# Four blocks of 32 array columns in place of two of 64 in the last FFN

## The chip, the cores and the metric

The kernel runs on one core of one Trainium2 chip. The metric is the device time of one execution in microseconds. Three runs of the kernel before gave 2269.03, 2269.31 and 2272.66 us; their median, 2269.31, is the time before.

## What is computed

The reference has two parts, all in fp32 at the outside: a long convolution whose filter comes from a small network, and a feed-forward network (FFN) that takes the maximum of three products.

```python
h_filt = (np.maximum(pos_emb @ w1, 0.0) @ w2) * np.exp(-0.01 * np.arange(S))[:, None]
y = irfft(rfft(x * v, n=2 * S) * rfft(h_filt, n=2 * S), n=2 * S)[:S]   # along S, for each batch
x = (x * y).reshape(B * S, 128)
h = np.maximum(np.maximum(x @ moe_w1, x @ moe_w2), x @ moe_w3)
out = h @ moe_w_out
```

There are 4 batches of S = 12544 positions and 128 channels; the FFN has 768 hidden units.

## The kernel before, in words

**The work.** The Fourier transforms are done as matrix products with tables. The filter's spectrum comes first, with batch 0; from then on the convolution of one batch runs beside the FFN of the batch before it. The FFN of the last batch has no convolution beside it any more. It is the part that the change touches, and it is called the last FFN here.

**The FFN.** A batch is cut into 32 tiles of N = 392 positions. For each tile the last stage of the inverse transform (`t_last`, L747-764) makes the 128 x 392 convolution result in PSUM by products with 49 columns each, and VectorE multiplies it by x into `gt`. Then, for each of the six groups of 128 hidden units, an up step (`up`, L766-775) makes two 128 x 392 products in two PSUM banks (tile name `hps`). The weights were changed beforehand to w2 - w1 and w3 - w1, so ScalarE takes relu of the first product, VectorE the maximum of that and the second (`hid`); the part x @ w1 @ w_out comes back as a product with `lin`. In batches 0 to 2 `down` (L777-789) multiplies by w_out.

**The last FFN** (the loop at the end of the kernel, and `products`, L823-882) takes tiles in pairs and saves products by a Strassen-like scheme over seven products: GpSimd makes sums of hidden tiles (`sum_`, L803), VectorE makes sums of weights once, and the small function `mm` (L832-836) issues the products. There a stationary operand has 64 columns, and it is used for both halves of a moving operand of 392 columns: the first half goes into the lower 64 output partitions, the second into the upper 64. `ORDER` fixes which up step comes when, `SUMS` and `LAG` place sums and products some steps later; `stream` holds what is due at which step. The loop issues an up step, then what is due. The last stage of the tiles two ahead is issued in the steps j = 5 and j = 8 of each pair. The first two tiles of the last FFN get their last stage earlier, while the other FFNs still run, and its first up step is issued before the loop too.

**How products use the array.** TensorE's array has 128 columns. `halves_mm` (L152-157) cuts a product with 128 output partitions into two instructions with 64 columns each, which use different column blocks of the array; up, down, the last stage and some products of the convolution all go through it, so their instructions all stand under L156. `mm` does the like at L834. A program's fp32 product shows in the trace as two weight loads (PEld) and two matmuls (PE), which are called records or passes here. Every product has its own weight load, and the queue of TensorE runs them in the program's order as far as their waits allow.

**Queues.** In the last FFN the loads are issued by SP, the stores by GpSimd (L858), four for each half of the output of a tile pair.

Of the kernel before, what the change touches and what calls it, by code (L numbers as in the profile page):

```python
# [16 lines left out]
P = 128  # L17
# [74 lines left out]
def kernel(  # L92
# [15 lines left out]
    nc = tc.nc  # L108
# [40 lines left out]

    copies = (nc.scalar.copy, nc.vector.tensor_copy)  # L150

    def halves_mm(out, lhsT, rhs, start, stop):  # L152


        for h in range(2):
            nc.tensor.matmul(out[64 * h:64 * h + 64], lhsT[:, 64 * h:64 * h + 64], rhs,  # L156
                             start=start, stop=stop, skip_group_check=True)

    def first_halves(ps, lhs, table, dsts, engines):
# [17 lines left out]
    def second(ps, w, g):  # L177

        for k in range(2):
            for r in range(2):  # L180
                halves_mm(ps[:, (2 * k + r) * D:(2 * k + r + 1) * D], w[:, k, r, :],
                          spec[:, 2 * g + k, r, :], k == 0 and r == 0, True)
# [127 lines left out]
    def warm_up(n):  # L310

        ps = next(turns_)
        for _ in range(n):
            halves_mm(ps[:, 0:256], warm[:, 0:P], warm[:], True, True)
# [279 lines left out]
    def g_third(g):  # L594
        w, ab = ws.pop((g, 1)), abs_.pop(g)
        ps = state["cv"][1].tile([P, 512], FP32, tag="cv", name="ps3")
        for k in range(2):
            for q in range(2):
                halves_mm(ps[:, (2 * k + q) * D:(2 * k + q + 1) * D], w[:, k, q, :],
                          ab[:, k, q, :], k == 0 and q == 0, True)  # L600
        if g < NK - 2:
            zs = state["cv"][0].tile([P, 2, 256], FP32, tag="z", name="zs", bufs=2)
        else:
            zs = lwp.tile([P, 2, 256], FP32, tag="w1", name="zs")
        nc.scalar.copy(zs[:].rearrange("p k f -> p (k f)"), ps[:])
        nc.sync.dma_start(
            zd[0][2 * g:2 * g + 2].rearrange("k c t f -> (c t) k f"), zs[:])
# [158 lines left out]
    def up(i, f, tag="hid", bufs=3):  # L766
        rhs = gs[i][:].rearrange("d p n -> d (p n)")
        h = (hidp if tag == "hid" else lp).tile([P, N], FP32, tag=tag, name="hid", bufs=bufs)
        pa = next(hbanks)
        halves_mm(pa[:, 0:N], w_sb[1][:, f * P:(f + 1) * P], rhs, True, True)  # L770
        nc.scalar.activation(h[:], pa[:, 0:N], Relu)  # L771
        pb = next(hbanks)
        halves_mm(pb[:, 0:N], w_sb[2][:, f * P:(f + 1) * P], rhs, True, True)
        nc.vector.tensor_tensor(out=h[:], in0=h[:], in1=pb[:, 0:N], op=ALU.max)  # L774
        return h

    def down(i, f, h):  # L777
        if f == 0:
            pos_[i] = ops.tile([D, 512], FP32, tag="ops", name="ops")
            halves_mm(pos_[i][:, 0:N], lin[:], gs[i][:].rearrange("d p n -> d (p n)"), True,  # L780
                      False)
        halves_mm(pos_[i][:, 0:N], wo_sb[:, f, :], h[:], False, f == NF - 1)
        if f < NF - 1:
            return
        gs.pop(i)
        o = op_.tile([D, 4, NB], FP32, tag="o", name="ot")
        nc.scalar.copy(o[:].rearrange("d p n -> d (p n)"), pos_.pop(i)[:, 0:N])  # L787
        dst = outT.rearrange("d (p b n) -> d p b n", b=B, n=NB)[:, 4 * i[1]:4 * i[1] + 4, i[0], :]
        nc.gpsimd.dma_start(dst, o[:])  # L789
# [5 lines left out]
    H2 = N // 2  # L795
# [27 lines left out]
    def products(b, i, h, X, Y):  # L823

        m1, m2 = lin[:, 0:64], lin[:, 64:128]
        first, second_ = gs[b, i], gs[b, i + 1]
        t = {}

        def new(name, bufs=1):
            return lp.tile([P, H2], FP32, tag=name, name=name, bufs=bufs)  # L830

        def mm(ps, w, rhs, start):  # L832
            for c in range(2):
                nc.tensor.matmul(ps[64 * c:64 * c + 64, 0:H2], w, rhs[:, H2 * c:H2 * c + H2],  # L834
                                 start=start, stop=True, skip_group_check=True)

        def place(name):

            if name[0] != "c":
                t[name] = new(name)  # L840
                return t[name][:]
            n, m = int(name[1]) - 1, int(name[2]) - 1
            if m not in t:
                t[m] = lp.tile([P, 2, H2], FP32, tag="o", name="o", bufs=2)
            return t[m][:, n]

        def copied(name, ps):
            nc.scalar.copy(place(name), ps[:, 0:H2])

        def added(name, a, ps):  # L850
            nc.vector.tensor_tensor(out=place(name), in0=t[a][:], in1=ps[:, 0:H2], op=ALU.add)  # L851

        def stored(m):
            dst = outT.rearrange("d (p b n) -> d p b n", b=B, n=NB)
            for n in range(2):
                for c in range(2):
                    at = 4 * (i + n) + 2 * c
                    nc.gpsimd.dma_start(  # L858
                        dst[64 * m:64 * m + 64, at:at + 2, b, :],
                        t[m][64 * c:64 * c + 64, n].rearrange("d (q n) -> d q n", q=2))  # L860

        plan = (
            (X, "h11", wo_sb[:, 0:NC, 0:64], True, None, [(copied, "p1", X)], None),
            (Y, "s2", tw[:, 0], True, None, [(added, "u2", "p1", Y)], None),
            (X, "h12", wo_sb[:, NC:, 0:64], False, (m1, first), [(copied, "c11", X)], None),
            (Y, "s3", tw[:, 1], False, (m2, second_), [(added, "u3", "p1", Y)], None),
            (X, "h21", wo_sb[:, 0:NC, 64:128], True, None, [(added, "c22", "u3", X)], None),
            (Y, "h22", tw[:, 2], True, (linx[:], second_), [(added, "c21", "u3", Y)],
             (stored, 0)),
            (X, "h12", wo_sb[:, NC:, 64:128], False, (m2, first), [(added, "c12", "u2", X)],  # L870
             (stored, 1)),
        )
        out = []
        for ps, name, w, start, extra, then, store in plan:
            for j in range(NC):
                out.append([lambda ps=ps, name=name, w=w, start=start, j=j: mm(
                    ps, w[:, j, :], h[name, j][:], start and j == 0)])
            if extra:
                out.append([lambda ps=ps, extra=extra: mm(ps, extra[0], extra[1][:].rearrange("d p n -> d (p n)"), False)])
            out[-1] += [lambda a=a: a[0](*a[1:]) for a in then]  # L880
            out[-1].append(store)
        return out
# [306 lines left out]
    for n, (b, i) in enumerate(tiles[:LAST]):  # L1189
# [21 lines left out]
        for f in range(NF):  # L1211
# [9 lines left out]
            h = up((b, i), f)  # L1221
# [18 lines left out]
    for l in late:  # L1240
        down(*l)
    conv.close()


    lp = ctx.enter_context(tc.tile_pool(name="lp", bufs=1))
# [20 lines left out]
    for i in range(0, NT, 2):  # L1266
        h = {}
        X, Y = banks if i % 4 == 0 else banks[::-1]
        for j, (name, f) in enumerate(ORDER):
# [6 lines left out]
            if step > 2 and weights:  # L1276
                out, a1, a2 = weights.pop(0)
# [59 lines left out]
```

## Time and profile before

| | us |
|---|---|
| time of the runs: median (lowest to highest of 3) | 2269.31 (2269.03 to 2272.66) |
| span of the profiled execution, first to last instruction | 2267.5 |
| first product of the last FFN to TensorE's last product | 1850.3 to 2260.1 |
| busy in that stretch: TensorE / its weight loads | 409.7 / 252.3 |
| busy in that stretch: VectorE / ScalarE / GpSimd | 196.5 / 104.4 / 265.1 |

The page gives the profiled execution only by its span; the median of the runs lies 1.8 us above it.

How to read the lines: a row of a group or of the timeline has the line of the kernel, the engine, the operation, the tile written and the tiles read, the shape, and the count. A shape such as `128*64 128x392 f32` is 128 rows and 64 columns of the array, and a moving operand of 128 partitions and 392 columns. PE stands for matmuls, PEld for weight loads. A row of the timeline begins with its start and its length in us; neighbours of one kind are merged, so that `x8` is eight matmuls. Durations of matmuls include the time that they take to run through the array, and they overlap; the distance between starts tells the pace.

### The profile page before, as it was taken

Reading aid. Unit: us, or ns where it says so; the run is one execution under the profiler, and the core shown is the slowest. Engines: PE = TensorE matmul, PEld = TensorE weight load, DVE = VectorE, ACT = ScalarE, POOL = GpSimd, SP = SyncE. Lnnn points to the kernel's source line nnn. Section 1 sums busy time; section 2 is a strip of 40 time slices with the busy share of each in tenths; the row PEclk is TensorE's granted clock in tenths of the full one; section 3 lists DMA queues with packets and bytes.
Section 4 is the critical chain, followed back from the end, with each engine's and each line's share of the span. In section 5 each row is a group of like instructions: output and inputs, shape, how many; then the busy total and the mean of one; then the engine's idle time right before and its main releaser. Section 6 shows DMA issues by size and latency. Waiting matters only on the chain.

```text
span 2267.5 us, 68405 instructions
## 1 busy us (share of the span) xinstructions
PE 2252.4 (99%) x27855; PEld 1356.9 (60%) x27855; DVE 1563.7 (69%) x2859; ACT 1176.0 (52%) x2131; POOL 876.7 (39%) x1090
## 2 busy tenths in 40 slices
PE   9999999999999999999999999999999999999998
PEld 8999866555555556655555556655555556666665
DVE  5589967678778667668888757667888754454443
ACT  3688844466666534456666534456666522222222
POOL 1145434223333234323333234323333326666666
PEclk9999999999999999999999999999999999999999
DMA  8788999889989599989999699889999732222221
GB/s 194 179 248 277 298 201 183 168 201 233 243 220 248 158 187 185 174 190 239 241 236 238 181 180 185 160 195 239 232 245 232 194 82 56 58 70 67 56 56 23
DMA packets 473324, 411.03 MB, mean 181 GB/s; under 512 B 327997, under 2 KB 374526, under 8 KB 473009
## 3 DMA queue, kind: packets, MB, share of 16 engines
q1 hardware_dynamic: 445929, 329.31, 64.4%
q0 software_dynamic: 26288, 75.62, 10.9%
q8 instruction: 219, 3.59, 0.7%
q10 hardware_dynamic: 792, 1.72, 0.3%
q14 instruction: 96, 0.79, 0.1%
HBM read 262.84 MB, written 84.67 MB: 153 GB/s over the span
## 4 chain that ended last, share of the span: by engine, by line
PE 99%; DMA 0%; issue 0%; ACT 0%; POOL 0%; DVE 0%; POOLq 0%; ACTq 0%; DVEq 0%
PE hps L156 45%; PE ops L156 20%; PE ops L834 6%; PE cps L428 5%; PE ps L156 4%; PE cps L156 4%; PE cps L496 3%; PE ps L165 3%; PE cps L506 3%; PE sps L1066 2%; PE gps L1048 2%; PE last L156 1%; PE ps L380 1%; PE ps L342 1%; DMA wt<-wt_const 0%; DMA zt<-zd 0%
## 5 line engine op out<-in xcount | busy, mean ns | idle before, releaser
L156 PE MATMUL hps<-gt,w_sb 128*64 128x392 f32 x6144 | 1146.2, 494 | 0.1
L771 ACT ACTIVATE hid<-hps 128x392 f32<-128x392 f32 x768 | 384.1, 500 | 699.6 <-PE hps L156 680.6
L156 PEld LDWEIGHTS hps<-gt,w_sb 128*64 128x64 f32 x6144 | 421.2, 137 | 430.8 <-issue 401.3
L774 DVE TENSOR_TENSOR hid<-hid,hps 128x392 f32<-128x392 f32 x768 | 428.0, 557 | 335.6 <-PE hps L156 323.0
L156 PE MATMUL ops<-hid,wo_sb 128*64 128x392 f32 x2304 | 477.1, 492 | 0.0
L548 POOL TENSOR_TENSOR cb<-cb,xs 128x512 f32<-128x512 f32 x135 | 173.9, 1288 | 474.7 <-DVE xs L545 384.1
L156 PEld LDWEIGHTS ops<-hid,wo_sb 128*64 128x64 f32 x2304 | 166.0, 137 | 213.1 <-issue 213.1
L521 DVE TENSOR_TENSOR cb<-cps,eo 128x512 f32<-128x512 f32 (+1 forms) x288 | 175.1, 649 | 76.1 <-ACT eo L518 76.1
L445 DVE TENSOR_TENSOR spec<-cps,high 128x360 f32<-128x360 f32 (+1 forms) x186 | 139.2, 789 | 104.7 <-ACT high L440 104.7
L789 POOL DMA_DIRECT2D out_dram<-ot x96 | 75.6, 788 | 335.2 <-ACT ot L787 282.3
L536 ACT ACTIVATE xs<-cb 32x512 f32<-32x512 f32 x270 | 169.6, 628 | 21.1 <-DVE cb L521 12.1
L537 ACT COPY xs<-cb 32x512 f32<-32x512 f32 x270 | 166.3, 616 | 3.2
L440 ACT COPY high<-cps 128x360 f32<-128x360 f32 x93 | 73.9, 797 | 169.7 <-PE cps L428 144.9
L552 DVE TENSOR_TENSOR xs<-cb 128x256 f32<-128x256 f32 x270 | 144.4, 580 | 7.7 <-POOL cb L548 7.7
L428 PEld LDWEIGHTS cps<-f1q,uT 98*64 98x64 f32 x2960 | 125.4, 137 | 26.2 <-issue 24.3
L428 PE MATMUL cps<-f1q,uT 98*64 98x90 f32 x2960 | 130.9, 241 | 0.0
L396 POOL COPY planes<-ut 128x784 uint16<-128x784 uint16 x90 | 76.3, 847 | 119.8 <-DVE ut L375 114.1
L529 POOL DMA_DIRECT2D zd<-cb x135 | 92.4, 685 | 63.7 <-DVE cb L521 60.7
L156 PEld LDWEIGHTS cps<-f4p,even 90*64 90x64 f32 x1552 | 87.5, 138 | 35.9 <-issue 34.6
L858 POOL DMA_DIRECT2D out_dram<-o x128 | 77.5, 610 | 51.5 <-DVE o L851 49.1
L156 PE MATMUL cps<-f4p,zt 90*64 90x49 f32 x1552 | 95.8, 222 | 0.0
L156 PE MATMUL cps<-f4p,even 90*64 90x49 f32 x1552 | 94.5, 220 | 0.0
(152 smaller groups left out, 3150.5 us busy)
## 6 DMA issues: line engine op xcount, KB each, us to landing
ht<-hd SPq DMA_DIRECT2D x264, 256.0 KB, 6.5
wt<-wq_const SPq DMA_DIRECT2D x144, 256.0 KB, 6.2
zd<-cb POOLq DMA_DIRECT2D x135, 256.0 KB, 5.7
zt<-zd SPq DMA_DIRECT2D x384, 90.0 KB, 3.0
sq<-spec SPq DMA_DIRECT2D x264, 128.0 KB, 6.4
ut<-in_xr_dram SPq DMA_DIRECT2D x128, 196.0 KB, 4.0
ut<-in_vr_dram SPq DMA_DIRECT2D x128, 196.0 KB, 4.4
xT<-in_x_dram SPq DMA_DIRECT2D x256, 98.0 KB, 3.4
```

The lines of the kernel that those rows point to most:

```text
L156: nc.tensor.matmul(out[64 * h:64 * h + 64], lhsT[:, 64 * h:64 * h + 64], rhs, start=start, stop=stop, skip_group_check=True)
L428: nc.tensor.matmul(ps[64 * c:64 * c + 64, 256 * i + h * N1:256 * i + (h + 1) * N1], t[:, 2 * ((at + i) % 8) + h].rearrange("n r t -> n (r ...
L445: nc.vector.tensor_tensor(out=spec[:, :, a, at:at + n], in0=v[:, 1], in1=highs[0], op=op)
L521: nc.vector.tensor_tensor(out=cb[:, a, lo:hi], in0=ps[:, lo:hi], in1=eo[:, lo:hi], op=op)
L529: nc.gpsimd.dma_start(zd[b][2 * z:2 * z + 2].rearrange("k c t a f -> (k c t) a f"), zss.pop(z))
L536: nc.scalar.mul(xs[at:at + 32], xt[at + 32:at + 64], -1.0)
L537: nc.scalar.copy(xs[at + 32:at + 64], xt[at:at + 32])
L548: nc.gpsimd.tensor_tensor(out=xts[g], in0=xts[g], in1=xs[:], op=ALU.add)
L552: nc.vector.tensor_tensor(out=ab[:, q], in0=y[:, 0], in1=y[:, 1], op=(ALU.subtract, ALU.add)[q])
L771: nc.scalar.activation(h[:], pa[:, 0:N], Relu)
L774: nc.vector.tensor_tensor(out=h[:], in0=h[:], in1=pb[:, 0:N], op=ALU.max)
L834: nc.tensor.matmul(ps[64 * c:64 * c + 64, 0:H2], w, rhs[:, H2 * c:H2 * c + H2], start=start, stop=True, skip_group_check=True)
```

## The change

A variable `block` holds the width of the column blocks. It is 64 up to the end of the convolution, and it is set to 32 just ahead of the last FFN's loop, so every product issued through `halves_mm` from there on (up steps and last stages) is four instructions with 32 columns each. `mm` is used in the last FFN alone, and it now issues four instructions as well: two blocks of 32 columns of the weights for each half of the moving operand. What is computed stays the same. Early last stages and the first up step of the last FFN, which are issued ahead of the switch, keep their two blocks.

```diff
+    block = [64]
+
     def halves_mm(out, lhsT, rhs, start, stop):
-        for h in range(2):
-            nc.tensor.matmul(out[64 * h:64 * h + 64], lhsT[:, 64 * h:64 * h + 64], rhs,
+        w = block[0]
+        for h in range(0, P, w):
+            nc.tensor.matmul(out[h:h + w], lhsT[:, h:h + w], rhs,
                              start=start, stop=stop, skip_group_check=True)
...
         def mm(ps, w, rhs, start):
-            for c in range(2):
-                nc.tensor.matmul(ps[64 * c:64 * c + 64, 0:H2], w, rhs[:, H2 * c:H2 * c + H2],
+            for q in range(4):
+                c, m = divmod(32 * q, 64)
+                nc.tensor.matmul(ps[32 * q:32 * q + 32, 0:H2], w[:, m:m + 32],
+                                 rhs[:, H2 * c:H2 * c + H2],
                                  start=start, stop=True, skip_group_check=True)
...
     conv.close()
+    block[0] = 32
```

## The prediction

> **What bounds the kernel now.** I read the page first: busy shares, then the chain of work that ended last. Then the stretch that the change touches, from the first product of the last FFN (1850.3 us) to TensorE's last product (2260.1 us): its busy time by engine, its TensorE groups by line and shape, and its timeline. From the page:
>
> ```profile
> PE 2252.4 (99%) x27855; PEld 1356.9 (60%) x27855; DVE 1563.7 (69%) x2859; ACT 1176.0 (52%) x2131; POOL 876.7 (39%) x1090
> ...
> PE 99%; DMA 0%; issue 0%; ACT 0%; POOL 0%; DVE 0%; POOLq 0%; ACTq 0%; DVEq 0%
> ```
>
> TensorE is the chain. The view by windows (stretch, PE, PEld, DVE, ACT, POOL busy, clock) says the same of the stretch: no idle TensorE, full clock, and no other engine over 65%.
>
> ```profile
> 1850.30:2260.10 409.80, 409.67 (x4072) 252.25 (x4068) 196.52 (x364) 104.36 (x221) 265.14 (x316) 1.00 0.22 56
> ```
>
> So only the pace of TensorE's own instructions counts. The groups from 1851 us on give three kinds of product (count, then busy us and mean ns of one):
>
> ```profile
> L156 PE MATMUL hps<-gt,w_sb 128*64 128x392 f32 x1508 | 280.2, 493 | 0.0
> L834 PE MATMUL ops<-hid,wo_sb 128*64 128x196 f32 x768 | 82.3, 329 | 0.0
> ...
> L156 PE MATMUL last<-f4p,zt 90*64 90x49 f32 x480 | 29.6, 222 | 0.0
> ```
>
> Every fp32 product of the program appears as two recorded matmuls (two passes). A duration is not a pace, for they overlap. The pace is in the timeline, by the starts of neighbouring rows:
>
> ```profile
> 2001.21 0.83 PE L834 MATMUL ops<-s,tw 128*64 128x196 f32 x8
> ...
> 2001.88 1.49 PE L156 MATMUL hps<-gt,w_sb 128*64 128x392 f32 x8
> ...
> 2003.19 0.50 PE L834 MATMUL ops<-gt,lin 128*64 128x196 f32 x4
> ...
> 2007.82 0.27 PE L156 MATMUL last<-f4p,even 90*64 90x49 f32 x4
> 2007.88 0.20 PEld L156 LDWEIGHTS last<-f4p,zt 90*64 90x64 f32 x4
> 2007.92 0.29 PE L156 MATMUL last<-f4p,zt 90*64 90x49 f32 x4
> ...
> 2008.62 0.29 PE L156 MATMUL last<-f4p,zt 90*64 90x49 f32 x4
> ...
> 2008.74 1.50 PE L156 MATMUL hps<-gt,w_sb 128*64 128x392 f32 x8
> ```
>
> I call a **round** one pass of all column blocks side by side, now two recorded matmuls. An up step has 4 rounds in 2003.19 - 1.88 = 1.31 us, 328 ns each. L834 has 4 in 0.67 us, 167 ns each. The last stage has 12 rounds from 2007.92 to 2008.62, 58.3 ns each, and 0.92 us in all.
>
> **What sets a round.** The mean durations 493 and 329 differ by 164 ns for 196 columns: 0.837 ns a column. So 392, 196 and 49 columns stream in 328, 164 and 41 ns. The first two rounds are pure streaming plus about 3 ns. The third is not: 41 against 58.3. What fits there is the weight load. A load of 64 columns takes 137 ns, one of 105 columns (L327) 171: 34 ns for 41 columns, 0.83 each, so 64 columns need 53 ns of loading, and 58.3 is that plus 5. A block can take its next weights only once its running product has let go of the buffer, so the period is the longer of (stream + 3) and (load + 5). That is my reading of these rows, not a shown rule.
>
> That column blocks really run side by side is seen in the filter's stage (L1048), where the two blocks have different weights and so different names:
>
> ```profile
> 116.21 0.32 PE L1048 MATMUL gps<-wt,specH 128*64 128x128 f32 x1
> 116.22 0.32 PE L1048 MATMUL gps<-wt,minus 128*64 128x128 f32 x1
> 116.37 0.27 PE L1048 MATMUL gps<-wt,specH 128*64 128x128 f32 x1
> 116.38 0.27 PE L1048 MATMUL gps<-wt,minus 128*64 128x128 f32 x1
> ```
>
> Both blocks start within 10 ns, then both second passes. Four blocks side by side are in the trace too, though as 64 rows by 64 columns (L506, with 128 columns to stream):
>
> ```profile
> 480.63 0.62 PE L506 MATMUL cps<-xs,wt 64*64 64x128 f32 x16
> 481.07 0.62 PE L496 MATMUL cps<-sq,wt 64*64 64x128 f32 x16
> ```
>
> 16 in 0.44 us are four rounds of 110 ns, 107 of them streaming: four run in the time of one.
>
> **The change, part by part.** It takes nothing away. Each product is cut into four blocks of 32 columns, each with its own load and both passes: load and matmul records of the stretch double, about 4,090 pairs to 8,180. DMAs, waits and the other engines' work stay.
>
> (1) *Up*: 191 steps (the first is issued before the switch) x 4 = 764 rounds; *L834*: 1600 recorded matmuls / 2 = 800 rounds. With four blocks at once a round still streams 328 or 164 ns; the loads get shorter and were hidden. Cost per round: L506's four blocks took 110 ns where L1048's two took 109 to 110 (116.70 to 116.81 to 116.92 us), so 0, give or take 1 ns: 1564 rounds, +-1.6 us. The far bounds: 3 ns gained (all that is not streaming), 4.7 us; or every round doubled (last rival). I take 0, by the nearest row. Pairs come every 41 ns in L834 after the change; L165 has 64 in 2.63 us, 41 ns each, so that pace is shown.
>
> (2) *Last stage*: the two tiles of the last FFN that run earlier stay as they are; 960 recorded matmuls / 32 = 30 tiles change, 16 rounds each. The load shrinks to 32 x 0.83 + 5 = 32 ns, so streaming rules: 41 + 3 = 44 ns. Gain 58.3 - 44 = 14.3 ns x 16 x 30 = **6.9 us**. Bounds of this cost: gain 16 x 30 x 17.3 = 8.3 us if not even 3 ns are left over; loss where pairs don't come fast enough, priced below.
>
> (3) Four blocks start some 20 ns after each other in place of 7 (L506's sixteen give about 7 ns a step), so ACT and DVE get a result 13 ns later. ACT has 305 us and DVE 213 us free in the stretch; without that cover it is 13 ns at each of 382 evictions, 5 us, but TensorE waits for none of them now. At the end it costs 13 ns once. Switching the array's form once is one drain, below 0.5 us by the first round's duration of 493 ns. What is late next if TensorE speeds up by 0.23 us in a tile of some 13 us: nothing near it; POOL, the busiest beside it, is at 65%.
>
> L506's four blocks start 7 ns apart, but the mean over its sixteen is 27.5 ns; no row of the trace shows a long run much closer than that. Here rules speak against (2). The Trainium skill, "TensorEngine Tiling (Array Packing)", Performance Considerations, gives each matmul about 60 cycles of overhead and says not to take a tiling factor from a dimension that is already small, as 49 columns are. Its page "TensorE: Matmul & The Clock Gate", Part 1, gives 25 ns as the least start-to-start of matmuls; by that, as an estimate, a tile's 64 pairs would take 1.6 us, and the change would cost 20 us where the sum above gains 6.9.
>
> **Sum.** 0 - 6.9 us on the profiled span of 2267.5: 2260.6. The median, 2269.31, lies 1.8 us above the span; so 2262.4.
>
> **Rivals.**
> *A, forecast: four at once, last stage falls to its stream.* For it: the rows of four blocks and the load's slope with the columns. Against: no row shows 128 rows by 32 columns, nor pairs 11 ns apart for long (44 / 4). 2262.4; from 2259.4 (8.3 us and the 1.6 of part 1 both gained) to 2264.
>
> *B, nothing moves.* The four loads of a round share two ways: 2 x 27 + 5 = 58 ns, as now; or the products lose 3 to 4 ns a round and give the gain back; or the blocks are not really cut to 32. All within 0.2% of 2269.3.
>
> *C, slower: TensorE is not fed fast enough in the last stage.* A tile needs 64 pairs of load and matmul instead of 32. The fastest long run is L342's: 64 pairs in 1.69 us (25.68 to 27.37), 26 ns each, though its weights are strided and its loads long (197 ns), which may be what sets that. About 17 pairs lie ready ahead: at 467.31 us TensorE's queue handles a wait for L506 while 17 pairs still run before it. So 47 pairs must arrive during the tile: 47 x 26 = 1.24 us against 0.92, +9.5 us in all, 2279; without the 17, 64 x 26 = 1.69, +23 us, 2292. It decides from 0.92 / 47 = 20 ns a pair upward. Against it: right after a wait that L342 ends at 16.67 us four of its pairs start within 20 ns.
>
> *D, slower: 128-row blocks run two at a time, not four*, because each must be fed with all 128 rows. L506's four share rows in twos, so no row excludes it. 764 x 0.328 + 800 x 0.167 = 384 us more, 2653 or above.
>
> **How the numbers follow.** A 0.52, B 0.20, C 0.20 (0.13 at its lower price, 0.07 at its upper), D 0.08. I predict A's time, 2262.4. A, B and C's lower price make 0.85, so the range runs from 2259.4 (A with all it could gain) to 2280; D and C's upper price lie outside. A's own range is 2259.4 to 2264. Changes of 0.2% (4.5 us) are about what a measurement of this kernel can tell from none: faster 0.52, same 0.20, slower 0.28.
>
> **What would show it.** In the profile after: 64-column loads of 137 ns become 32-column loads near 110; up steps still 1.31 us, L834's groups still 0.67; a last-stage tile 0.70 instead of 0.92 with four starts per round 44 ns apart. C would show last-stage tiles of 1.2 us and more, even or slowing after the first 17 pairs; D up steps of 2.6 us, with starts in twos. I am wrong if rounds of up or L834 grow by more than 3 ns, or if loads don't shrink with their columns.

## The result, and the profile after

The changed kernel takes 2263.74 us (median of 8 runs, 2262.47 to 2265.41) against 2269.86 us for the kernel before (8 runs): 6.1 us less, a ratio of 0.9973 with a 95% interval of 0.9963 to 0.9983. The forecast was 2262.4. The profiled execution has a span of 2261.7 us against 2267.5.

First the page, then the view by windows for the stretch of the last FFN (TensorE, its weight loads, VectorE, ScalarE, GpSimd busy, clock, DMA share):

```profile
PE 2247.3 (99%) x31943; PEld 1347.9 (60%) x31943; DVE 1563.8 (69%) x2859; ACT 1176.1 (52%) x2131; POOL 878.0 (39%) x1090
```

```profile
1850.30:2254.30 404.00, 403.49 (x8148) 242.28 (x8140) 197.18 (x365) 104.61 (x222) 266.94 (x317) 1.00 0.23 58
```

The stretch starts at 1850.3 us, as in the profile before; the last FFN's loop itself starts some 3 us earlier in the traces, with its first product at 1847.40 us before and 1847.76 after. In the stretch the records have doubled (8148 against 4072), as the diff says, yet it is shorter, 404.0 us against 409.8. Weight loads are busy 242 us, less than the 252 of before, though there are twice as many. The groups of the stretch, by line and shape, tell what a load costs now (busy us, mean ns):

```profile
L159 PEld LDWEIGHTS hps<-gt,w_sb 128*32 128x32 f32 x3012 | 104.1, 110 | 79.6 <-issue 68.4 <-ACT o L853 1.9 <-DVE hid L777 1.5
...
L159 PE MATMUL last<-f4p,even 90*32 90x49 f32 x960 | 24.4, 206 | 0.0
```

A load of 32 columns takes 110 ns where one of 64 took 137. Last-stage matmuls end a little sooner (206 against 222 ns), and their busy time falls by a sixth. The timeline (start, length, and so on) gives the pace:

```profile
1859.76 0.27 PE L159 MATMUL last<-f4p,zt 90*32 90x49 f32 x8
1859.85 0.27 PE L159 MATMUL last<-f4p,even 90*32 90x49 f32 x8
1859.94 0.27 PE L159 MATMUL last<-f4p,zt 90*32 90x49 f32 x8
1860.03 1.50 PE L159 MATMUL hps<-gt,w_sb 128*32 128x392 f32 x16
1861.35 1.18 PE L838 MATMUL ops<-hid,wo_sb 128*32 128x196 f32 x24
1862.34 1.50 PE L159 MATMUL hps<-gt,w_sb 128*32 128x392 f32 x16
```

Eight matmuls of the last stage are two rounds of four blocks. They start 88 ns apart, 44 ns a round, where two blocks needed 58. The up step still takes 1.32 us (1860.03 to 1861.35) and L838, six rounds here, 0.99 us, 165 ns each. So four blocks of 128 rows run side by side, and the gain comes from the last stage. Adding up the loop from the starts in the two traces (each group of products up to the start of the next), last stages take 27.6 us before and 21.2 after, final products 126.1 and 126.1 (their last group left out), up steps 252.1 and 252.3.

The 0.2 us more in the up steps are a gain and two waits. The first round of an up step after a last stage comes 13 ns sooner than before (most such up steps take 1.319 us in place of 1.332), 0.37 us in all. The first wait is at 1857 us. Rows of the timeline show it (in square brackets the idle time before a row, and what ended it):

```profile
1857.38 0.55 DVE L777 TENSOR_TENSOR hid<-hid,hps 128x392 f32<-128x392 f32 x1
...
1857.98 0.16 PEld L159 LDWEIGHTS hps<-gt,w_sb 128*32 128x32 f32 x8 [0.80 <-DVE hid L777]
```

VectorE's `hid`, the maximum that frees a bank, ends at 1857.93, and the next up step's loads start behind it. The three up steps from 1855.07 take 4.25 us; before, they took 4.02. The second wait is for GpSimd (POOL):

```profile
2166.04 0.60 POOL L863 DMA_DIRECT2D out_dram<-o  x1 [2.09 <-issue]
2166.66 1.04 POOL L807 TENSOR_TENSOR s<-hid 128x392 f32<-128x392 f32 x1
...
2168.61 2.43 POOL L863 DMA_DIRECT2D out_dram<-o  x4
2171.06 1.03 POOL L807 TENSOR_TENSOR s<-hid,s 128x392 f32<-128x392 f32 x1
```

GpSimd stands 2.09 us at issuing a store, as it does in the kernel before at the same place, and its sum lands late. Before, the up step there came out 0.09 us longer than its neighbours; now, with TensorE earlier, it is 0.40 us longer, and the products after it wait for the sum:

```profile
2172.14 0.54 PE L838 MATMUL ops<-s,tw 128*32 128x196 f32 x8 [0.20 <-POOL s L807]
```

### The profile page after: what moved, and what is told of

Read it like the earlier page. It is cut to its first block, busy times and chain, and to the rows that moved or that the text cites. A ratio compares the mean times of both kernels' runs of the same rounds, so it can differ in the third digit from the quotient of the medians.

```text
span 2261.7 us, 76581 instructions
## 1 busy us (share of the span) xinstructions
PE 2247.3 (99%) x31943; PEld 1347.9 (60%) x31943; DVE 1563.8 (69%) x2859; ACT 1176.1 (52%) x2131; POOL 878.0 (39%) x1090
## 4 chain that ended last, share of the span: by engine, by line
PE 98%; POOL 0%; issue 0%; DMA 0%; DVE 0%; ACT 0%; POOLq 0%; DVEq 0%; ACTq 0%
PE hps L159 45%; PE ops L159 20%; PE ops L838 6%; PE cps L431 5%; PE ps L159 4%; PE cps L159 4%; PE cps L499 3%; PE ps L168 3%; PE cps L509 3%; PE sps L1071 2%; PE gps L1053 2%; PE last L159 1%; PE ps L383 1%; PE ps L345 1%; POOL out_dram L863 0%
## 5 line engine op out<-in xcount | busy, mean ns | idle before, releaser
L159 PE MATMUL hps<-gt,w_sb 128*64 128x392 f32 (+1 forms) x7672 | 1150.8, 494 | 0.2
L159 PEld LDWEIGHTS hps<-gt,w_sb 128*64 128x64 f32 (+1 forms) x7672 | 419.2, 126 | 432.8 <-issue 401.7
L159 PE MATMUL ops<-hid,wo_sb 128*64 128x392 f32 x2304 | 477.2, 492 | 0.0
L159 PEld LDWEIGHTS ops<-hid,wo_sb 128*64 128x64 f32 x2304 | 166.3, 137 | 212.9 <-issue 212.9
L539 ACT ACTIVATE xs<-cb 32x512 f32<-32x512 f32 x270 | 169.6, 628 | 21.2 <-DVE cb L524 12.2
L431 PEld LDWEIGHTS cps<-f1q,uT 98*64 98x64 f32 x2960 | 125.6, 137 | 26.1 <-issue 24.2
L431 PE MATMUL cps<-f1q,uT 98*64 98x90 f32 x2960 | 130.9, 241 | 0.0
L159 PEld LDWEIGHTS cps<-f4p,even 90*64 90x64 f32 x1552 | 87.5, 138 | 35.8 <-issue 34.7
L159 PE MATMUL cps<-f4p,zt 90*64 90x49 f32 x1552 | 95.8, 222 | 0.0
L159 PE MATMUL cps<-f4p,even 90*64 90x49 f32 x1552 | 94.6, 220 | 0.0
```

The source lines that it names most:

```text
L159: nc.tensor.matmul(out[h:h + w], lhsT[:, h:h + w], rhs, start=start, stop=stop, skip_group_check=True)
L431: nc.tensor.matmul(ps[64 * c:64 * c + 64, 256 * i + h * N1:256 * i + (h + 1) * N1], t[:, 2 * ((at + i) % 8) + h].rearrange("n r t -> n (r ...
L539: nc.scalar.mul(xs[at:at + 32], xt[at + 32:at + 64], -1.0)
```

## The experiments

The prediction's reading is called theory L below: a block's round is the longer of its own stream and its own weight load. The kernel before ran beside each experiment; its medians were 2270.3 to 2271.0 us.

**1. The last stage alone in four blocks.** Two of 64 stay in the up steps and in `mm` (the edit of `mm` is taken back too). Edits are shown by their main lines: against the changed kernel, in 7 against the kernel before, in 8 against 6 and in 9 against 7.

```diff
-    block[0] = 32
+    last[0] = True
...
+                halves_mm(y[:, s, a * h:a * h + h], ..., range(0, P + 1, 32) if last[0] else None)
```

> Only the last stages of the last FFN go to four blocks of 32; up steps and the final products keep two of 64. Theory L (a block's round is the longer of its stream + 3 ns and its own weight load + 5 ns, so the gain is all in the last stage): a last-stage tile takes 0.70 us in place of 0.92, 30 tiles gain 6.5 us; but the array's form now changes 60 times, and the one change of form in the changed kernel's timeline took about 0.10 us (1847.66 to 1847.76), so 6 us go back: within 2 us of the kernel before. If changes of form cost nothing: 6.5 us faster, as the whole change. Rival S (the gain comes from the up steps and the final products): no gain, or 6 us slower.

It took 2271.63 us, ratio 1.0011 (1.0003 to 1.0020): 1.3 us slower than before, not 6 faster. The timeline shows both halves of the account:

```profile
2011.19 0.83 PE L838 MATMUL ops<-hid,tw 128*64 128x196 f32 x8
2011.95 0.29 PE L159 MATMUL last<-f4p,even 90*32 90x49 f32 x8
...
2012.59 0.27 PE L159 MATMUL last<-f4p,zt 90*32 90x49 f32 x8
2012.79 1.54 PE L159 MATMUL hps<-gt,w_sb 128*64 128x392 f32 x8
2014.16 0.50 PE L838 MATMUL ops<-hid,tw 128*64 128x196 f32 x4
```

After the first, the rounds are nearly as fast as in the changed kernel (45 ns). But L838's four rounds should end at 2011.85 (0.66 us), and the last stage starts 0.10 later; from 2011.95 it should be done by 2012.65, and the up step starts 0.14 later and then takes 1.37 us, not 1.32. A pair of changes of form costs 0.29 us by these rows and 0.26 by the time (1.3 + 6.45 us over 30 tiles), more than the 0.215 us that a tile gains.

**2. The products alone in four blocks.** Up steps and `mm` as in the changed kernel, the last stage in two blocks of 64.

```diff
-                halves_mm(y[:, s, a * h:a * h + h], ...)
+                halves_mm(y[:, s, a * h:a * h + h], ..., (0, 64, 128) if last[0] else None)
```

> Only up steps and final products of the last FFN go to four blocks of 32; its last stages keep two of 64. Theory L: no gain in the products (rounds of 329 and 166 ns as before), last-stage tile 0.92 us, and 60 changes of form at 0.10 us: about 6 us slower than before, or the same if changes of form cost nothing. Rival S: the gain of 6 us is here, so 6 us faster, or the same after the changes of form.

2278.4 us, ratio 1.0037 (1.0025 to 1.0050), 8.1 us slower. Up steps and final products have the same medians as before, 1.317 and 0.663 us, so there is no gain in them; a last-stage tile takes 1.07 us to the next product instead of 0.92. The slowdown is the changes of form, 0.135 us each where 0.10 was expected. Rival S falls. The two runs together say why the change needed the products too: they gain nothing, but left at 64 they take the last stage's gain away.

**3. Does the load set the round?** The same four blocks, but their 32 weight columns are taken 16 elements apart.

```diff
-                halves_mm(y[:, s, a * h:a * h + h], zt[a][:, s * D:(s + 1) * D], ...)
+                for q in range(4):
+                    nc.tensor.matmul(y[32 * q:32 * q + 32, s, a * h:a * h + h],
+                                     zt[a].rearrange("k (m c) -> k c m", c=16)[:, 4 * s + q], ...)
```

> The changed kernel, but each last-stage block takes its 32 weight columns 16 elements apart instead of next to each other (the transform's output is permuted by it, so the result is another one; instructions, blocks and columns are the same). Theory L: loads of spread columns are longer (41 columns, 128 elements apart, took 197 ns of which some 84 are fixed, 2.8 ns a column); at that price 32 columns take 88 ns, the round becomes 93 ns, a last-stage tile 1.5 us, and the kernel 23 us slower than the changed one. Rival N (58 ns was a fixed turnaround that four blocks share better than two, whatever the loads take): rounds stay at 44 ns, tile 0.70 us, no change of time.

One run, 2271.76 us, 8 us slower than the changed kernel. The view of the tile `last` (lowest, median and highest duration in ns) and the timeline:

```profile
L766 PEld LDWEIGHTS last<-f4p,zt x960: 134/162/183, 1854.4 to 2225.8; 90*32 90x32 f32 x192
```

```profile
1855.01 0.32 PE L766 MATMUL last<-f4p,zt 90*32 90x49 f32 x8
1855.14 0.33 PE L766 MATMUL last<-f4p,even 90*32 90x49 f32 x8
1855.27 0.33 PE L766 MATMUL last<-f4p,zt 90*32 90x49 f32 x8
1855.40 1.84 PE L159 MATMUL hps<-gt,w_sb 128*32 128x392 f32 x20
```

Loads go from 110 to about 160 ns, and rounds with them from 44 to 65 ns here, with instructions, blocks and columns unchanged. So longer loads make longer rounds, and rival N falls. The size was off: expected were rounds of 93 ns and 23 us more than the changed kernel. Even the 50 ns by which loads did grow should have made 82 ns by "load + 5"; the median tile, 1.00 us, shows 63. So "load + 5" does not carry over to strided weights, and why is not shown.

**4. Two of the four blocks.** The upper half of the last stage's outputs is left out.

```diff
-                halves_mm(y[:, s, a * h:a * h + h], ...)
+                halves_mm(y[:, s, a * h:a * h + h], ..., (0, 32, 64) if last[0] else None)
```

> The changed kernel, but a last stage computes only its first two blocks of 32 columns; output partitions 64 to 127 are left out (they stay zero). Theory L (a block's pace is set by its own stream and its own load): rounds stay at 44 ns with two blocks as with four, tile 0.70 us, time as the changed kernel. Rival N (it takes four blocks to hide a turnaround of 58 ns): two blocks fall back to 58 ns, tile 0.92 us, 6.5 us slower than the changed kernel.

One run, 2262.61 us, span 2260.8. The timeline, where two rounds are now `x4`:

```profile
1858.61 0.26 PE L159 MATMUL last<-f4p,even 90*32 90x49 f32 x4
1858.70 0.26 PE L159 MATMUL last<-f4p,zt 90*32 90x49 f32 x4
1858.79 0.26 PE L159 MATMUL last<-f4p,even 90*32 90x49 f32 x4
```

44 ns a round with two blocks of 32 as with four. Against the 58 ns of two blocks of 64, with as many instructions and the same stream, only the columns of a block differ: what counts is how many columns a block loads, not how many blocks there are. The tile takes 0.63 us to the next product, not 0.70, as that product's first matmuls start (1859.23) ahead of the tile's last two (1859.27).

**5. A shorter stream.** Each last-stage product streams 24 columns.

```diff
-                halves_mm(y[:, s, a * h:a * h + h], ..., f4p[..., a, :], ...)
+                halves_mm(y[:, s, a * h:a * h + 24], ..., f4p[..., a, 0:24], ...)
```

> The changed kernel, but each last-stage product streams 24 of its 49 columns (the other columns of the result are left out and stay zero). A round's stream shrinks to 20 + 3 = 23 ns. Theory L: now the load of 32 columns rules, 27 + 5 = 32 ns a round, tile 0.51 us, 5.8 us faster than the changed kernel. If loads of 32 columns had no such bound: 23 ns a round, tile 0.37 us, 10 us faster. If TensorE cannot take 64 pairs at 8 ns: the tile stays above 0.55 us, and the rounds get longer after the first 17 pairs.

One run, 2259.48 us, span 2257.7, 4.3 us less than the changed kernel's median. In the trace the median round is 33 ns, where the stream alone would allow 23: the round is the one expected from the load of 32 columns. A limit of some 8 ns on each pair of load and matmul would give the same 33 ns for four blocks, though, and no run here has pairs coming faster for long, so this run alone does not tell the two apart. Tiles took 0.56 us rather than 0.51: the first round took 47 ns, and some 35 ns were lost once in the middle of each tile. Before that the pairs came 8 ns apart, after it 8.3, so feeding did not break down after the first 17.

**6. Every FFN in four blocks.** By theory L there are 98 more tiles with 0.215 us each to gain, 21 us, if nothing changes form in between. So the switch moves ahead of the FFN of batch 0, and L431 is cut in four as well (L432 in this run's rows).

```diff
+    block[0] = 32
     besides, plans = {}, []
...
-                for c in range(2):
+                for q in range(0, P, block[0]):
+                    c, m = divmod(q, 64)
...
-    block[0] = 32
```

> Every FFN from batch 0 on, its last stages, and the first transform's products beside it (line 431, 90 columns) go to four blocks of 32. Theory L: 96 + 2 more last-stage tiles gain 0.215 us each, 21 us, on top of the 6: about 27 us faster than before, 2243 us, if transfers and the other engines keep up; the transform's rounds stay 78 ns since 90 columns stream longer than 64 are loaded. Rival S or a gain that belongs to the last FFN alone: no more than the 6 us of the whole change. If TensorE cannot be fed 128 pairs at 19 ns beside the transform: slower than the changed kernel.

2305.57 us, ratio 1.0156 (1.0142 to 1.0170): 35 us slower. Tiles of the last stage did take 0.705 us, and L431's groups 1.24 us as before. Most of the loss is in waits of TensorE that nothing in the profile explains ("issue"). The view of waits (us in total, times, longest), the timeline, and a window:

```profile
PE hps L159 <- issue: 10.0, 7, 3.8
PE cps L432 <- issue: 8.3, 7, 2.4
PE cps L501 <- issue: 8.1, 7, 3.2
```

```profile
983.10 1.28 PE L432 MATMUL cps<-f1q,uT 98*32 98x90 f32 x52
986.78 0.43 PE L432 MATMUL cps<-f1q,uT 98*32 98x90 f32 x10 [2.40 <-issue]
```

```profile
400.00:600.00 200.00, 190.15 (x3746) 108.41 (x3742) 135.07 (x239) 105.13 (x191) 54.66 (x60) 0.97 0.86 194
```

A group of products breaks off in the middle, with no semaphore in it, and goes on 2.4 us later. In 39 such waits TensorE stands still 39 us from 300 to 1950 us; before, 0.1. Nearly all waits over 0.3 us end about 1.45 us after a 16 KB packet of the instruction queue has landed (441.56 then 443.15; 494.06 then 495.60). After some of the longer waits the granted clock falls besides, to 0.97 over this window; from 300 to 1950 us it is 0.99, where it was 1.00 before.

**7. More instructions in the old form.** In experiments 7 to 9 theory F says that instructions arrive too late, and rival C, not the C of the prediction, that the loss belongs to the new form and its changes. This is the kernel before, but in the FFNs of batches 0 to 2 each product's 392 moving columns are streamed as two times 196.

```diff
-            nc.tensor.matmul(out[64 * h:64 * h + 64], lhsT[:, 64 * h:64 * h + 64], rhs, ...)
+            for at in range(0, n, n // 2): ...
+                nc.tensor.matmul(out[64 * h:64 * h + 64, at:at + n // 2], ..., rhs[:, at:at + n // 2], ...)
```

> The kernel before, with two blocks of 64 throughout, but in the FFNs of batches 0 to 2, beside the convolution, every product of 392 columns is cut into two of 196: matmuls and loads of these FFNs double, blocks and forms of the array stay. It tells why the run with all FFNs at 32 lost 35 us. Theory F (instructions come by DMA in 16 KB packets, and beside the convolution's transfers they come too late for twice as many): 3648 more rounds at 2.8 ns cost 10 us, and on top TensorE stands still some 20 to 40 us in waits ascribed to issue, each ending about 1.5 us after such a packet lands: 2300 to 2320 us. Rival C (the loss was changes of the array's form between 128 by 32 and 64 by 64): 10 us and no standstill: 2280 us.

2282.21 us, ratio 1.0052 (1.0035 to 1.0069), 11.9 us slower, with 2.0 us of standstill. That looked like rival C. But this kernel asked for only 16.1 pairs a microsecond (counted from 320 to 1800 us), the one of experiment 6 for 19.6. It left the question open.

**8. Every FFN, but L431 in two blocks.** As 6, without its edit of L431:

```diff
-                for q in range(0, P, block[0]):
-                    c, m = divmod(q, 64)
+                for c in range(2):
```

> As the run with all FFNs at four blocks of 32, but the first transform's products beside them (line 431) keep two of 64. Theory F (the standstill of 39 us in that run came of matmuls and loads asked for faster than their instructions arrive, above all in the transform's bursts at 19 ns a pair): the pace is now about that of the run with a split moving operand, which stood still 2 us, so no more than 5 us of standstill; against it some 100 groups of line 431 now bring two more changes of form each at 0.135 us, 26 us; last stages gain 27 us in all; sum near 2270 to 2280 us. Rival C (the standstill comes with the 32-column form beside the convolution): standstill of 20 us or more, 2295 us or above.

2297.77 us, ratio 1.0111 (1.0094 to 1.0128), with 20.5 us of standstill at 17.7 pairs a microsecond. By its numbers this was a point for rival C, and theory F as I had put it, no more than 5 us, missed. So one more run had to part form from pace.

**9. Still more instructions in the old form.** As 7, but the up steps' columns are cut in four.

```diff
-            for at in range(0, n, n // 2): ...
+            for at in range(0, n, n // 4 if start and stop else n // 2): ...
```

> The kernel before with two blocks of 64 throughout; in the FFNs of batches 0 to 2 the up steps' products are cut into four of 98 columns, the down products into two of 196. Array forms stay, but TensorE is asked for more pairs of load and matmul than in the run with all FFNs at 32 but line 431 (per tile about 280 against 216, beside the same convolution). 8300 more rounds at 2.8 ns cost 23 us, 2294 us. Theory F (standstill comes of the pace at which instructions are asked for, whatever the form): 20 us of standstill or more, with the clock falling behind it, 2315 us or above. Rival C (standstill belongs to the 32-column form beside the convolution): no more standstill than the 2 us of the run with the split moving operand, 2292 to 2297 us.

One run, 2340.62 us, span 2338.8, with 29.3 us of standstill at 21.2 pairs a microsecond:

```profile
PE hps L161 <- issue: 17.9, 14, 2.2
PE cps L161 <- issue: 2.6, 5, 0.8
```

All blocks of the FFNs have 64 columns here, so the 32-column form is not needed for the standstill, and rival C falls. Of this run's 70 us over the kernel before, 29 are standstill and 23 were forecast for the added rounds; the rest was not parted. The table has all of them beside the convolution; the last row is the changed kernel's last FFN, where transfers take a quarter of the DMA engines instead of nine tenths.

| | columns of a block | pairs per us | standstill us |
|---|---|---|---|
| before | 64 | 11.5 | 0.1 |
| 7 | 64 | 16.1 | 2.0 |
| 8 | 32 (L431: 64) | 17.7 | 20.5 |
| 6 | 32 | 19.6 | 39.0 |
| 9 | 64 | 21.2 | 29.3 |
| changed kernel, last FFN | 32 | 20.2 | none ascribed to issue |

Beside the convolution TensorE begins to run out of instructions somewhere from 16 to 18 pairs a microsecond, if both forms are taken together; in the old form alone, between 16.1 and 21.2. The mean pace does not order the runs fully: 6 stood still longer than 9, so bursts or the form may add to it. That instructions arrive late because of the other transfers is inferred from the packets that end the waits and from the last row; no run took the transfers away. Experiment 6 lost 35 us where 27 were to be gained: 39 of these 62 us are standstill, the clock accounts for some 12 more by an estimate (in the trace it is halved six times, 23.9 us in all), and the rest was not parted further.

## Why the prediction was right

**Products at no cost (part 1): right.** Medians of 1.317 and 0.663 us before and after, and experiment 2, which has the change in them alone, shows no gain.

**The last stage (part 2): right in mechanism, a little large.** The round of 44 ns was met (705 ns a tile, 704 forecast). The term of 6.9 us was 6.45 by tiles, 30 x (0.920 - 0.705): I multiplied the steady round's gain by 16, but the first round of each tile before took only 48 ns, so there was less to save. The up steps' first rounds after the tiles gave 0.37 us that the sum did not have. Experiments 3 and 4 show what had only been argued from two load durations, that the load of a block's own columns set the old round of 58 ns; that the load rules again at 33 ns (experiment 5) is not parted from a limit per pair.

**What is late next (part 3): wrong in two places.** I named nothing, since no other engine was busy for more than 65% of the stretch. VectorE's `hid` at 1857 us took back 0.24 us, and GpSimd's sum at 2171 us 0.3 us. The loop gets shorter by 6.24 us, from 412.24 (1847.40 to TensorE's last product at 2259.64) to 406.00 (1847.76 to 2253.76): 6.4 in the last stages and 0.37 behind them, less 0.54 in the two waits. The last product starts only 5.88 us earlier in the trace, for the loop starts 0.36 us later: 0.10 is the change of form below, and 0.26 the two executions already differ by at 1846 us, ahead of everything that was changed. So the forecast gain of 6.9 us was 0.45 too large in the tiles and lacked these small terms (0.54 and 0.10 lost, 0.37 won); with them it would have been some 6.2 us, near the 6.1 that the medians show.

**The one change of form**, below 0.5 us, cost 0.10: L159's old form starts its eight matmuls at 1846.34, four rounds of 329 ns end at 1847.66, and the new form begins at 1847.76.

```profile
1846.34 1.49 PE L159 MATMUL ops<-hid,wo_sb 128*64 128x392 f32 x8
1847.76 6.79 PE L159 MATMUL hps<-gt,w_sb 128*32 128x392 f32 x80
```

**Rivals.** D fell with the up step at 1.32 us. B fell with the load at 110 ns and the round at 44. C was priced for a place where it does not happen: 64 pairs came 11 ns apart, 9 ns in experiment 5, against the 26 ns that L342 suggested. That L342's strided weights made those rows slow is likely but not shown: strided weights slow other products in experiment 3, there to 16 ns a pair. The least start-to-start of 25 ns, which the Trainium skill gives in "TensorE: Matmul & The Clock Gate", Part 1, does not hold between blocks of different columns here. The rule against a tiling factor from a small dimension, which the prediction held against part 2, does not speak of this change: the factor comes out of the 128 columns of the weights, and the 49 streamed columns stay whole. But C's mechanism is seen elsewhere: beside the convolution TensorE does run short of instructions, 39 us in experiment 6.

No version tried here that computes the whole result beats the changed kernel; experiments 4 and 5 are shorter by what they leave out.

## What to carry to other kernels

Where a product streams fewer columns than its weights take to load, cut the weights into narrower blocks: each block is paced by its own load, and blocks run side by side (58 to 44 ns a round here). Keep neighbouring products in the same form of the array, even those that gain nothing, since two changes of form cost more than a tile of 16 rounds gained. And count the instructions: doubling them was free in the last FFN, where the DMA engines were a quarter busy, and went with a loss of 35 us beside a convolution that kept them nine tenths busy.

## What the runs showed that I had not expected

The four blocks do not start evenly 7 ns apart, as the prediction had them. In the middle of an up step two start together, and the other two 40 and 45 ns later (2002.068, 2002.068, 2002.108 and 2002.113 us); it costs nothing, as the median up step stays at 1.317 us.

A change of form costs about 0.10 to 0.14 us: 128 by 64 to 128 by 32 and back in experiments 1 and 2. In the kernel before, changes to 64 by 64 and back beside the convolution cost about 0.10 (median start-to-start 422 ns where two up rounds lie 322 apart).

A wait for instructions can cost twice, by itself and by the clock. In experiment 6 the granted clock fell six times, with waits of 1.3 to 3.8 us, but not after each of that length: from 980 to 1000 us, with a wait of 2.4 us in it, it stayed at 1.00. The window from 850 to 870 us has a wait of 2.0 us in it, and a granted clock of 0.91:

```profile
850.00:870.00 20.00, 17.98 (x403) 11.66 (x399) 11.13 (x20) 6.75 (x13) 6.53 (x9) 0.91 0.95 178
```
